# Output stores on another queue, a last tile in three parts, and weight pieces issued at other steps, in a hash-attention and gated feed-forward kernel

## The chip, the core and the metric

The kernel runs on one core of a Trainium2 chip. The metric is the device time of the whole program in microseconds (us), the median of five runs. The core has five engines with an instruction queue each: TensorE (PE in the profile), VectorE (DVE), ScalarE (ACT), GpSimd (POOL) and SyncE (SP). Each queue is worked off in its written order. DMA transfers are issued from SP, ACT and POOL and are carried by 16 DMA engines.

## The reference

For each of 4 batches and 8 heads, with 768 tokens of 64 features, queries and keys get a 6-bit bucket from the signs of a projection. A query attends only to keys of its own bucket. Then follows a gated feed-forward part on 3072 tokens of 512 features.

```python
q_bits = (np.einsum('bhsd,dk->bhsk', q, proj) > 0)
k_bits = (np.einsum('bhsd,dk->bhsk', k, proj) > 0)
mask = q_bucket[:, :, :, None] == k_bucket[:, :, None, :]
scores = np.where(mask, scale * np.matmul(q, k.transpose(0, 1, 3, 2)), -1e9)
x = softmax(scores) @ v                      # heads side by side: 3072 x 512
g, val = x @ w_gate, x @ w_val               # 512 -> 1536
ffn_out = (gelu(g) * val) @ w_out            # 1536 -> 512
out = x + sigmoid(x @ w_res) * ffn_out
```

## The kernel before, in words

The work is cut into eight blocks: 4 batches times 2 halves of 384 query tokens. In a block the 8 heads are taken as 4 pairs. A pair of a block has 6 steps; a block has 24.

One step computes scores for 2 key tiles of 128 and 384 queries (`scores`, L563 to L583): two matmuls into the double-buffered `sc`, and one exponential on ACT into `e`. The bucket mask is part of the matmul: `aug` holds, per head pair, 64 feature rows and 7 rows of bits, so that a pair of different buckets gets a very negative score. `attend` (L585 to L625) multiplies `e` with `vaug` (values with a column of ones) into the single-buffered `av`. After the sixth step of a pair DVE takes the reciprocal of the sums (L615) and writes the pair into `xtok` (L616); only then can the next pair use `av`. From the second block on, each pair's `xtok` is transposed by a DMA of the SP queue into `xT` (L624); in the first block PE does it (L638).

At the end of a block, `gate` (L648 to L661) multiplies `xT` with `wg` (12 column groups of 4 matmuls, L656) and ACT applies the gelu. `feed_forward` (L663 to L715) then multiplies with `wv` (L672), which DVE multiplies into `gh` (L675). For each of 3 token tiles there follow the gate product with `wr` (L684, ACT L687), 12 matmuls with `wo` (L697), two DVE operations into `y` and `o` (L705, L708), and the store of the tile (L714). In the last tile of the last block the 512 columns are done as two parts of 256. The feed-forward of one block is mixed between the attention steps of the next.

Head pairs reach `aug` in two ways. In the first batch (`prep_tokens`, L385 to L518) tokens are transposed on PE (L470, L494), the result is taken out of PSUM with a scale into `trT` (L395), hashed with a matmul (L457), turned into bits on DVE (L421), and moved into `aug` (L431), beside a cast of the features (L409 to L413). The table `EVAC` says which engine does the three takings-out of pairs 1 to 3: ACT for all. In later batches (`prep_blocks`, L520 to L552) tokens are loaded in pieces of 32 columns (L266), transposed on DVE (L526), hashed (L534), turned into bits (L541), and the bits are moved by DMAs of the POOL queue (L544). `cast_v` (L380), also on POOL, makes `vaug`.

The weights come through the POOL queue in 13 pieces (L361: `wg` 4, `wv` 4, `wr` 1, `wo` 4), with a cast on the way. The token loads of the second batch on SP wait until `wr` is there: `wait_weights` (L282) puts a tiny DMA in front of them that reads `wr` (L283).

What stands where in each queue is settled when the program is built. `arrange` (L136 to L257) is a planner: every operation has an engine, an estimated cost, its dependencies, its buffers (rings of the sizes in `RINGS`), and marks such as `margin` (an addition to the time at which it is taken to be ready). The planner plays this through and emits the operations in the order in which they start. Where PE has nothing to do during the first 35 us of the plan, it emits matmuls that do no useful work (L823, L826). So a change of one cost or one engine can move other instructions too.

Of the kernel before, what the change touches and what calls it, by code (L numbers as in the profile page):

```python
# [11 lines left out]
FP32 = mybir.dt.float32  # L12
# [8 lines left out]
def kernel(  # L21
# [12 lines left out]
    nc = tc.nc  # L34
    B, H, S, D = q.shape
# [34 lines left out]
                 th=2, y=2, o=2, rec=2)  # L70
# [312 lines left out]
    EVAC = [None] + [("ACT",) * 3] * 3  # L383

    def prep_tokens(n):  # L385
# [13 lines left out]
        def cast(eng, par, hhs, sides, after=()):  # L399
# [4 lines left out]
            def emit():  # L404
                do = {"DVE": nc.vector.tensor_copy, "ACT": nc.scalar.copy}[eng]
# [8 lines left out]
            op(eng, {"DVE": 0.16 + width * 0.00053, "ACT": 0.12 + width * 0.00088}[eng], emit,  # L414
               r=[(trT, hh, side) for hh in hhs for side in sides],
               w=[("aug", n % NAUG, hh, side, par, "d") for hh in hhs for side in sides], after=after)
# [46 lines left out]
        if n == 0:  # L463
            for hh in range(2):
                for side in range(2):
# [7 lines left out]
                    op("PE", 0.35, emit, r=[(st[side], hh)], w=[ps], margin=0.3 if hh else 0.0)  # L473
# [11 lines left out]
        else:  # L485

            tiles = [(hh, side, t2) for hh in range(2) for side in range(2) for t2 in range(TC)]
            for g in range(3):
# [8 lines left out]
                op("PE", 0.45, emit, r=[(st[side], 0) for side in range(2)], w=[ps], margin=0.4)  # L497
# [7 lines left out]
            for par in range(2):  # L505
                bit(hp, par, (0, 1))
            cast("DVE", 0, (0, 1), (0, 1))
            for hh in range(2):
                move(hh, 0, (0,))
                move(hh, 1, (0, 1))  # L510
                if hh == 0:
                    cast("DVE", 1, (0, 1), (1,))
# [150 lines left out]
    def feed_forward(u):  # L663
# [14 lines left out]
        for t in range(TC):  # L678
# [10 lines left out]
            parts = 2 if u == 2 * B - 1 and t == TC - 1 else 1  # L689
            W = DMODEL // parts  # L690
            for h in range(parts):
                cols = slice(h * W, (h + 1) * W)
                ps = bank()
                for k4 in range(KF // 4):
# [4 lines left out]
                    op("PE", 0.87 / parts, emit, r=[(g, kk) for kk in range(4 * k4, 4 * k4 + 4)] + [("wo", gg) for gg in range(KF // 3)],  # L699
# [3 lines left out]
                y = ring("y", [P, DMODEL], FP32)  # L703
                o = ring("o", [P, DMODEL], FP32)
                op("DVE", 0.66 / parts, lambda y=y, th=th, ps=ps, cols=cols, W=W: nc.vector.scalar_tensor_tensor(  # L705
                    y()[:, 0:W], th()[:, cols], 1.0, ps()[:, 0:W], op0=ALU.add, op1=ALU.mult), r=[th, ps], w=[y],
                   closes=("block", u + 1) if t == TC - 1 else None)
                op("DVE", 0.68 / parts, lambda y=y, o=o, t=t, cols=cols, W=W: nc.vector.scalar_tensor_tensor(  # L708
# [5 lines left out]
                op("SP", 0.5, lambda o=o, dst=dst, W=W: nc.sync.dma_start(dst, o()[:, 0:W]), r=[o], size=0.8)  # L714
# [13 lines left out]
    ahead = {0: (0, 0, 1, 1), 2: (2,), 5: (2,), 8: (3,), 11: (3,)}  # L728
    for i in range(LB):
# [5 lines left out]
        if i % 2 == 0:  # L735
            next(weights)
# [129 lines left out]
```

## Time and profile before

| quantity | us |
|---|---|
| median of 5 runs | 351.37 |
| lowest and highest of them | 349.91, 352.73 |
| the profiled execution's own time | 352.71 |
| its span, first to last instruction | 350.9 |
| PE busy in the span | 339.7 |
| ACT busy | 235.1 |
| DVE busy | 189.8 |
| POOL busy | 51.3 |

The span is what the profile's times count from. Some 1.8 us of the profiled execution lie outside it. A busy PE is not PE at its peak: matmuls are pipelined and their ends are modelled. Lines beginning with "PEld" are weight loads, which overlap matmuls. "SPq" and "POOLq" are the queues of these engines with their DMA issues.

### The profile page before, as it was taken

What the parts mean: (1) busy time and instruction counts of PE and PEld (TensorE: products, weight loads), DVE (VectorE), ACT (ScalarE), POOL (GpSimd) and SP (SyncE); (2) the same over time, 40 slices, a digit from 0 to 9 for tenths busy, and PEclk for the clock granted to TensorE, in tenths of its full rate; (3) what the DMA queues carried; (4) which work ended last, traced back from release to release, by engine and by line L of the source; (5) the groups of instructions that cost most, each with busy time, mean ns of one, the idle gap of its engine ahead of it and who ended that gap; (6) DMA issues with size and microseconds to landing.
All of it is one profiled execution on the core that took longest, in us unless ns stands there. A gap on an engine that the chain in (4) does not pass through costs nothing.

```text
span 350.9 us, 7702 instructions
## 1 busy us (share of the span) xinstructions
PE 339.7 (97%) x3073; PEld 202.5 (58%) x3097; DVE 189.8 (54%) x339; ACT 235.1 (67%) x341; POOL 51.3 (15%) x83
## 2 busy tenths in 40 slices
PE   8998999997999999999999999999999999999995
PEld 3666666454565556655666556555665556655653
DVE  3897137968389746896263534734162414423353
ACT  4789887653866758675876768685787758775410
POOL 0634000331234200302002100202000000000000
PEclk9999999998999999999999999999999999999999
DMA  7979999999987299863501120021000120012002
GB/s 225 350 156 186 206 152 160 136 156 177 185 138 125 67 184 151 144 140 81 111 12 19 45 75 2 16 55 48 30 13 13 43 73 0 20 48 71 2 0 90
DMA packets 117557, 34.23 MB, mean 98 GB/s; under 512 B 107786, under 2 KB 113554, under 8 KB 117522
## 3 DMA queue, kind: packets, MB, share of 16 engines
q1 hardware_dynamic: 112402, 27.78, 43.1%
q0 software_dynamic: 4816, 5.77, 9.2%
q8 instruction: 24, 0.39, 0.5%
q10 hardware_dynamic: 304, 0.20, 0.2%
q14 instruction: 11, 0.09, 0.1%
HBM read 29.36 MB, written 6.29 MB: 102 GB/s over the span
## 4 chain that ended last, share of the span: by engine, by line
PE 92%; DVE 4%; ACT 2%; DMA 1%; issue 1%; ACTq 0%
PE mm L656 18%; PE mm L672 18%; PE mm L697 18%; PE sc L574 16%; PE av L602 9%; PE mm L684 6%; PE mm L534 3%; ACT e L578 2%; DVE bits L421 1%; DVE aug L431 1%; PE idle L823 1%; DMA xT<-xtok 1%; PE mm L494 1%; PE mm L470 1%; PE av L826 1%
## 5 line engine op out<-in xcount | busy, mean ns | idle before, releaser
L578 ACT ACTIVATE e<-sc 128x768 bf16<-128x768 f32 x192 | 149.4, 810 | 52.4 <-PE sc L574 52.2
L675 DVE TENSOR_TENSOR gh<-mm,gh 128x384 bf16<-128x384 f32 x96 | 53.3, 556 | 79.9 <-PE mm L672 65.7
L574 PE MATMUL sc<-aug 71*128 71x384 bf16 x384 | 93.2, 327 | 1.0 <-ACT e L578 0.7
L672 PE MATMUL mm<-xT,wv 128*128 128x384 bf16 x384 | 73.5, 326 | 0.0
L602 PEld LDWEIGHTS <-e 128*128 128x128 bf16 x1152 | 57.1, 97 | 23.4 <-PE mm L494 1.1
L656 PE MATMUL mm<-xT,wg 128*128 128x384 bf16 x384 | 67.5, 330 | 2.6 <-DMA xT<-xtok 2.4
L697 PE MATMUL mm<-wo,gh 128*128 128x512 bf16 (+1 forms) x291 | 69.0, 371 | 0.4
L660 ACT ACTIVATE gh<-mm 128x384 bf16<-128x384 f32 x96 | 45.4, 490 | 34.8 <-PE mm L656 34.5
L602 PE MATMUL av<-vaug,e 128*128 128x65 bf16 x1152 | 62.4, 194 | 1.3 <-DVE xtok L616 1.3
L656 PEld LDWEIGHTS <-wg 128*128 128x128 bf16 x384 | 37.4, 99 | 28.4 <-issue 4.4
L574 PEld LDWEIGHTS <-aug 71*128 71x128 bf16 x384 | 34.8, 99 | 29.3 <-issue 5.7
L672 PEld LDWEIGHTS <-wv 128*128 128x128 bf16 x384 | 34.0, 98 | 21.5 <-issue 3.1
L544 POOL DMA_DIRECT2D aug<-bits x48 | 27.1, 570 | 103.3 <-DVE bits L541 103.1
L697 PEld LDWEIGHTS <-gh 128*128 128x128 bf16 x300 | 26.9, 98 | 26.1 <-issue 1.9
L705 DVE SCALAR_TENSOR_TENSOR y<-th,mm 128x512 f32<-128x512 bf16 (+1 forms) x25 | 16.6, 665 | 46.8 <-PE mm L697 41.7
L380 POOL CAST vaug<-vs 128x768 bf16<-128x768 f32 x16 | 15.4, 965 | 87.3 <-DMA vs<-in_v_dram 58.5
L687 ACT ACTIVATE th<-mm 128x512 bf16<-128x512 f32 x24 | 14.3, 597 | 16.6 <-PE mm L684 16.6
L549 DVE TENSOR_SCALAR aug<-trT 64x1536 bf16<-64x1536 f32 x24 | 23.4, 975 | 1.1 <-PE sc L574 0.4
L684 PE MATMUL mm<-wr,xT 128*128 128x512 bf16 x81 | 22.9, 380 | 0.8
L541 DVE TENSOR_SCALAR bits<-mm,shift 128x384 bf16<-128x384 f32 x24 | 13.6, 609 | 10.4 <-PE mm L534 10.3
L616 DVE TENSOR_TENSOR xtok<-av,rec 128x384 bf16<-128x384 f32 x32 | 17.8, 557 | 1.1
L708 DVE SCALAR_TENSOR_TENSOR o<-y,xtok 128x512 f32<-128x512 f32 (+1 forms) x25 | 17.1, 685 | 0.9
(54 smaller groups left out, 152.3 us busy)
## 6 DMA issues: line engine op xcount, KB each, us to landing
vs<-in_v_dram SPq DMA_DIRECT2D x16, 384.0 KB
out_dram<-o SPq DMA_DIRECT2D x23, 256.0 KB
qs<-in_q_dram SPq DMA_DIRECT2D x48, 96.0 KB
ks<-in_k_dram SPq DMA_DIRECT2D x48, 96.0 KB
wg<-in_moe_w_gate_dram POOLq DMA_DIRECT2D x4, 384.0 KB, 8.1
wv<-in_moe_w_val_dram POOLq DMA_DIRECT2D x4, 384.0 KB, 6.7
wo<-in_moe_w_out_dram POOLq DMA_DIRECT2D x4, 384.0 KB, 14.9
qs<-in_q_dram SPq DMA_DIRECT2D x3, 384.0 KB
```

Of the source, the lines that this page charges most:

```text
L544: op("POOL", 0.6, lambda i=i: nc.gpsimd.dma_start(a[D:KAUG, :, i * CH:(i + 1) * CH], bits()[32 * i:32 * i + NR]), r=[(bits, 0), (bits, 1)] ...
L549: lambda hh=hh: nc.vector.tensor_scalar_mul(a[0:D, hh, :], trT()[hh * D:(hh + 1) * D].rearrange("d s n -> d (s n)"), QKS),
L574: nc.tensor.matmul(sp()[:, x, 0:CH], a[:, S + jt * P:S + (jt + 1) * P], a[:, c * CH:(c + 1) * CH], start=True, stop=True)
L578: op("ACT", 0.72, lambda: nc.scalar.activation(e(), sp()[:, :, 0:CH], AF.Exp, scale=EXPS), r=[sp], w=[e], table="exp", held=True, opens=(" ...
L602: nc.tensor.matmul(av()[:, o:o + D + 1], e()[:, x, t * P:(t + 1) * P], va[:, 2 * j + hh, TS[b][jt], :], start=(first and x == 0 and t == 0 ...
L616: op("DVE", 0.48, lambda: nc.vector.tensor_mul(xt()[:, j].rearrange("p t (h d) -> p h t d", h=2), view()[:, :, :, 0:D], rec().to_broadcast ...
L656: nc.tensor.matmul(ps()[:, 0:CH], wg[:, kk, m * P:(m + 1) * P], x()[:, kk, :], start=(kk == 0), stop=(kk == KM - 1))
L660: op("ACT", 0.385, lambda: nc.scalar.activation(g()[:, m, :], ps()[:, 0:CH], AF.Gelu), r=[ps], w=[(g, m)], table="gelu", closes=("gelu", u ...
L672: nc.tensor.matmul(ps()[:, 0:CH], wv[:, kk, m * P:(m + 1) * P], x()[:, kk, :], start=(kk == 0), stop=(kk == KM - 1))
L675: op("DVE", 0.46, lambda m=m, ps=ps: nc.vector.tensor_mul(g()[:, m, :], ps()[:, 0:CH], g()[:, m, :]), r=[ps], w=[(g, m)])
L684: nc.tensor.matmul(rps(), x()[:, kk, t * P:(t + 1) * P], wr[:, kk, :], start=(kk == 0), stop=(kk == KM - 1))
L697: nc.tensor.matmul(ps()[:, 0:W], g()[:, kk, t * P:(t + 1) * P], wo[:, kk, cols], start=(kk == 0), stop=(kk == KF - 1))
```

## The change

1. The stores of blocks 1 to 7 (21 stores of 128 x 512) are issued from the POOL queue. Those of the last block stay on SP.
2. The last tile of the last block is done in parts of 256, 128 and 128 columns, with buffers `yz` and `oz` of their own, three each.
3. The 13 weight pieces are planned at steps 3, 4, 6, 7, 9, 10, 12, 13, 15, 16, 18, 19 and 21 of the first block, where they were planned at every second step from 0 to 24.
4. In pairs 1 to 3 the second of the three takings-out of `trT` is done by DVE (`EVAC`).
5. Margins change: for the transposes of the keys of head 1 of pair 0 from 0.3 to 1.3, and of pairs 1 and 2 from 0.4 to 1.4.
6. Planner costs of the two last DVE operations and of the store change. The tables `MOVER` and `CASTER` are new and name DVE everywhere, as before.

```diff
-    EVAC = [None] + [("ACT",) * 3] * 3
+    EVAC = [None, ("ACT", "DVE", "ACT"), ("ACT", "DVE", "ACT"), ("ACT", "DVE", "ACT")]
+    MOVER = ["DVE", "DVE", "DVE", "DVE"]
+    CASTER = [None, ("DVE", "DVE"), ("DVE", "DVE"), ("DVE", "DVE")]
...
-                    op("PE", 0.35, emit, r=[(st[side], hh)], w=[ps], margin=0.3 if hh else 0.0)
+                    op("PE", 0.35, emit, r=[(st[side], hh)], w=[ps], margin=(0.3, 1.3)[side] if hh else 0.0)
...
-                op("PE", 0.45, emit, r=[(st[side], 0) for side in range(2)], w=[ps], margin=0.4)
+                op("PE", 0.45, emit, r=[(st[side], 0) for side in range(2)], w=[ps], margin=(None, 1.4, 1.4, 0.4)[n])
...
-            parts = 2 if u == 2 * B - 1 and t == TC - 1 else 1
-            W = DMODEL // parts
-            for h in range(parts):
-                cols = slice(h * W, (h + 1) * W)
+            parts = [256, P, P] if u == 2 * B - 1 and t == TC - 1 else [DMODEL]
+            for h, W in enumerate(parts):
+                cols = slice(sum(parts[:h]), sum(parts[:h]) + W)
...
-                y = ring("y", [P, DMODEL], FP32)
-                o = ring("o", [P, DMODEL], FP32)
-                op("DVE", 0.66 / parts, lambda ...
+                z = "z" if len(parts) > 1 else ""
+                y = ring("y" + z, [P, parts[0]], FP32)
+                o = ring("o" + z, [P, parts[0]], FP32)
+                op("DVE", 0.1 + 0.56 * W / DMODEL, lambda ...
...
-                op("SP", 0.5, lambda o=o, dst=dst, W=W: nc.sync.dma_start(dst, o()[:, 0:W]), r=[o], size=0.8)
+                eng, queue = ("SP", nc.sync) if u == 2 * B - 1 else ("POOL", nc.gpsimd)
+                op(eng, 0.6, lambda o=o, dst=dst, W=W, queue=queue: queue.dma_start(dst, o()[:, 0:W]), r=[o], size=0.8)
...
+    WSTEPS = (3, 4, 6, 7, 9, 10, 12, 13, 15, 16, 18, 19, 21)
...
-        if i % 2 == 0:
+        if i in WSTEPS:
             next(weights)
```

## The prediction

> **What bounds the kernel now.** I read the page's busy times first, then PE's waits, the stage table, and the queues around the largest wait.
>
> ```profile
> span 350.9 us, 7702 instructions
> PE 339.7 (97%) x3073; PEld 202.5 (58%) x3097; DVE 189.8 (54%) x339; ACT 235.1 (67%) x341; POOL 51.3 (15%) x83
> ```
>
> PE is idle for only 11.2 us in all, so a gain must come from those, from useless or slow PE work, or from the two ends. PE's waits have one large entry:
>
> ```profile
> PE mm L656 <- DMA xT<-xtok: 2.4, 1, 2.4
> PE av L602 <- DVE xtok L616: 1.3, 2, 0.9
> ```
>
> The stage table around it (length, busy time and count of PE, PEld, DVE, ACT, POOL; then PE's granted clock, DMA share, GB/s):
>
> ```profile
> 78.00:80.00 2.00, 0.82 (x5) 0.39 (x4) 1.69 (x3) 0.00 (x0) 0.00 (x0) 1.00 1.18 298
> 80.00:82.00 2.00, 0.80 (x3) 0.41 (x3) 1.99 (x2) 0.00 (x0) 1.39 (x1) 0.76 0.69 195
> 82.00:85.00 3.00, 3.00 (x19) 1.57 (x18) 2.93 (x5) 0.40 (x2) 0.00 (x0) 0.59 0.82 133
> ```
>
> The wait ends at 81.2, and the clock is low until about 85: the stall costs more than its 2.4 us. It is at the gate of block 2, which needs the transposes of pairs 3 and 4. The SP queue then:
>
> ```profile
> 75.99 0.73 SPq L266 DMA_DIRECT2D vs<-in_v_dram  x1
> 76.83 1.17 SPq L714 DMA_DIRECT2D out_dram<-o  x1
> 78.09 1.23 SPq L624 DMA_TRANSPOSE xT<-xtok  x1
> 79.42 0.52 SPq L714 DMA_DIRECT2D out_dram<-o  x1
> 80.03 1.20 SPq L624 DMA_TRANSPOSE xT<-xtok  x1
> ```
>
> Pair 3 was in `xtok` at 68.2, but its transpose was issued at 78.09, behind loads and a store. SP issues without a pause from 38.16 to 81; what started it is SP's longest early wait:
>
> ```profile
> SPq L283 <- DMA wr<-in_moe_w_res_dram: 10.2, 1, 10.2
> ```
>
> POOL and the DMA engines before that (timeline, then a stage row):
>
> ```profile
> 23.43 1.36 POOL L380 CAST vaug<-vs 128x768 bf16<-128x768 f32 x1 [6.01 <-DMA vs<-in_v_dram]
> 24.73 2.19 POOL L361 DMA_DIRECT2D wv<-in_moe_w_val_dram  x4
> 26.87 0.81 POOL L361 DMA_DIRECT2D wr<-in_moe_w_res_dram  x1
> ...
> 24.00:26.00 2.00, 2.00 (x40) 1.13 (x25) 1.95 (x4) 1.32 (x3) 2.00 (x4) 1.00 0.12 23
> ```
>
> `wv` and `wr` stand behind a cast that waits for the fourth `vs`; meanwhile the DMA engines run dry (share 0.12). After 85 each stage of about 40 us has 0.15 us of idle PE, so only the first 85 us and the tail can change much.
>
> **The change part by part.** *Weight pieces.* In the changed program POOL's queue reads: cast, cast, `wg`, cast, three `wg`, cast, then `wv`, `wr`, `wo`; before it was cast, two `wg`, two casts, two `wg`, cast. So the first two pieces, issued at 11.36 to 12.6, fall behind the casts of the second and third `vs`: estimate 14.3 and 15.8. Until then the token loads have the DMA engines alone. Stage rows put 3.25 MB into SBUF by 12 us; the tokens of the first batch are 12 x 393 KB = 4.72 MB; the rest at the 396 GB/s of 10 to 12 us takes 3.7 us, plus some 1.5 us to land: the fourth `vs` is there at about 17 instead of 23.4, and `wv` is issued from about 18.5. Then no gap forms. Between 22.5 and 26 the finer rows are 178, 89, 61, 0, 49 and 131 GB/s in slices of 0.75 us, where a `wg` or `wv` stream makes 215: (6 - 508/215) x 0.75 = 2.7 us lost. So `wr` lands at 38.2 - 2.7 = 35.5 and the SP chain starts 2.7 us earlier. Bounds: no gain, if the total is set by something else, and 3.9 us, from counting bytes at full rate. I take 2.7. `wg` itself lands near 25 and is first used at about 38, `wv` at 46: covered.
>
> *Stores.* SP loses 1.17 + 0.52 us and two gaps of 0.09: the transpose of pair 3 moves up 1.26 us for the store alone, that of pair 4 1.87 us. With the chain 2.7 us earlier pair 3 is issued at 78.1 - 1.3 - 2.7 = 74.1; pair 4 must wait for its `xtok` (76.0 before, 75.6 below), so it is issued at 75.7 and, at 3.1 us from issue to use as in the chain of waits (78.09 3.07), lands at 78.8. PE, now with all four score matmuls ahead, comes to the gate at 78.4 and needs pair 4 after nine matmuls of 0.163, at 79.8. Margin 1 us: the stall is gone. Worth: from the start of the last `wo` group (75.41) to the long gate run (85.14) it is 9.73 us; in block 3, where nothing stalls, 121.79 to 127.17 = 5.38, plus 0.19 for six `av` matmuls that lie elsewhere. Saving 9.73 - 5.57 = **4.2 us**.
>
> [...] The rows show 0.76 and 0.59 after a 2.4 us wait; they decide, and I keep 4.2.
>
> POOL pays 21 issues. Nearest row, also from POOL:
>
> ```profile
> L544 POOL DMA_DIRECT2D aug<-bits x48 | 27.1, 570 | 103.3 <-DVE bits L541 103.1
> ```
>
> 21 x 0.6 = 13 us on an engine that spends 103 us waiting for bits. What is queued behind a store are the `vaug` casts and these bit moves. [...] L544 took at most 0.89 here beside busy DVE. [...]
>
> *DVE for ACT in the first block.* ACT loses 3 x 0.60 us (L395). DVE gains three of about 0.69 (L395 at 384 columns is 0.552 and L705 grows from 0.42 to 0.686 for 256 columns). Neither counts alone, because DVE closes each pair (L615, L616) after it has done the next pair's bits. Walking the new order with the old durations (exponential 0.74 apart, cast 0.95 and 0.56, two bits 1.14, four moves 1.3, closing 0.8):
>
> ```profile
> 15.75 1.14 DVE L421 TENSOR_SCALAR bits<-mm,shift 128x384 bf16<-128x384 f32 x2
> 16.93 1.32 DVE L431 COPY aug<-bits 7x384 bf16<-7x384 bf16 x4
> ...
> 22.64 0.56 DVE L616 TENSOR_TENSOR xtok<-av,rec 128x384 bf16<-128x384 f32 x1
> ```
>
> The key transposes of head 1 now stand behind a hash that waits for `proj` until 7.45, so the first exponential slips from 10.3 to about 11.1. The moves of pair 2 end at 18.4 (18.25 before), exponential 8 is done at 20.7 (21.1), number 11 starts at 23.7 (25.2). Then DVE's extra work tells: pair 1 is closed at 24.1 (23.2), number 13 starts at 25.7 (26.7); pair 2 is closed at 29.6 (28.95), number 19 starts at 31.2 (31.6). Eight more at 0.74 and the last end at 37.8 instead of 38.18: **-0.4 us**. Bounds: -1.8, if all of ACT's time were a gain, and +2.1, if all of DVE's were a loss. [...]
>
> *Tail.* Two halves took 2.78 us of PE; 12 matmuls of 256 (1.39) and 24 of 128 (0.061 each, as the 116-column L826) make 2.85. DVE then is the limit: with 0.285 for a 128-column operation its last one ends at 347.95, before at 347.91. A smaller last store may give 0.1 back. **0**; bounds -0.3 and +0.3.
>
> **Sum.** -4.2 - 0.4 + 0 = -4.6 on a span of 350.9 gives 346.3; with the 1.8 us around it the profiled execution's 352.71 becomes 348.1. That execution was 1.3 us above the median; on the median of 351.37 the same difference gives **346.8 us**.
>
> **The rivals.** *Store and loads share the DMA engines (B).* The chain from 38.16 on is paced by transfers, and `wr` lands as late as before because bytes are bytes. [...] For it: DMA shares over 1 in 55 to 75. Against: 298 GB/s at 78 to 80, so 125 to 160 is not full, and the gap at 24 to 26.
>
> *The gate of the loads opens later (C), slower.* Place: the SP wait on `wr`. The first pieces are issued 3 to 4 us later; if that lateness goes through the 13-piece queue instead of filling the gap, `wr` lands at 42, the chain moves +3.8, the stores give back 1.3, and the transpose is 2.5 us later: 353.9. It decides from `wr` at about 39.5. Against: the old order itself left the engines empty.
>
> *DVE becomes the bound of the first block (D).* The stall goes, but the first block is 2.1 us longer: 351.4 - 4.2 + 2.1 = 349.3. For it: DVE was busy 22.0 of 28.35 us there. *The whole 1.8 us of ACT is gained (E):* 345.4.
>
> **How the numbers follow.** Chances: the main case 0.55, B 0.19, C 0.12, D 0.08, E 0.06. Half a per cent, 1.76 us, is about what a measurement of this kernel can tell from no change: the bounds are 349.6 and 353.1. Faster: main, E, D and a part of B, 0.72; same: most of B and a little of C, 0.17; slower: 0.11. The main case alone spans 345.0 to 348.9, from the bounds of the first block. For 8 in 10 the range takes in D and most of B, and a little of E: 344.7 to 350.9. C is left out.
>
> **What would show it.** `wv` issued near 18.5 to 20 and SP's tiny read of `wr` near 35.5; no wait of L656 for `xT` and no slice of low clock near 80; the first gelu table load near 37.8; `aug` issues still under 0.9 us; last DVE operation 3 us before the end. The prediction is wrong if `wr` lands at 38 or later, if the fourth `vs` still lands after 20, or if the first exponentials fall into groups with gaps over 1 us.

## The result

The changed kernel takes 349.84 us (median of 43 executions, 348.41 to 352.04) against 350.4 us of the kernel before (80 executions, 348.01 to 354.02): a ratio of 0.9983, interval 0.9969 to 0.9996. Forecast were 346.8 us and a range of 344.7 to 350.9. The time lies in the range, but the gain is 0.6 us where 4.6 were forecast, so the forecast was wrong in size: a gain of over one per cent was forecast, and what came can hardly be told from none. A ratio is not the quotient of the two medians, and it leaves out executions more than 1.5% above the fastest of their kernel.

The profiled execution of the changed kernel took 349.84 us. Lines of the changed kernel have other numbers: L581 is the scores, L585 the exponential, L609 `attend`, L623 the closing of a pair, L631 the transpose, L663 the gate, L703 the `wo` matmuls, L722 the store. From its page, the head and the busy times:

```profile
span 348.0 us, 7654 instructions
PE 335.8 (96%) x3044; PEld 199.6 (57%) x3068; DVE 191.9 (55%) x344; ACT 233.7 (67%) x338; POOL 64.5 (19%) x104
```

POOL has the 13 us of stores that were forecast, and PE is idle for 12.2 us, 1.0 us more than before, although the span is 2.9 us shorter. PE's waits, largest first (total, times, longest, us):

```profile
PE mm L663 <- DMA xT<-xtok: 2.6, 2, 1.8
PE sc L581 <- ACT e L585: 1.4, 5, 0.4
PE av L609 <- DVE xtok L623: 1.2, 1, 1.2
PE sc L581 <- DVE aug L434: 0.4, 1, 0.4
```

In this execution the wait for the transposed pair is not gone. It is one wait of 1.8 us in place of 2.4, and a second one of 0.8 us has come. The stage rows around the first (columns as in the prediction):

```profile
78.00:80.00 2.00, 0.22 (x2) 0.00 (x0) 1.93 (x4) 1.76 (x2) 0.94 (x2) 1.00 1.13 84
80.00:82.00 2.00, 2.00 (x23) 1.34 (x23) 1.99 (x2) 0.50 (x2) 0.46 (x1) 1.00 1.16 233
82.00:85.00 3.00, 3.00 (x25) 1.83 (x21) 2.93 (x4) 2.22 (x5) 0.00 (x0) 1.00 1.34 161
```

PE has 0.22 us of work from 78 to 80, but the clock stays at 1.00 behind it. That gives most of the shorter span of this execution: from the first gate matmul to the long gate run the chain of waits has 45.05 us (37.43 to 82.48) against 46.92 before, and the low rows of before had cost (1 - 0.76) x 2 + (1 - 0.59) x 3 = 1.7 us of PE's time. The SP queue (start, duration):

```profile
72.42 0.46 SPq L266 DMA_DIRECT2D vs<-in_v_dram  x1
72.98 3.08 SPq L631 DMA_TRANSPOSE xT<-xtok  x1
76.15 2.29 SPq L631 DMA_TRANSPOSE xT<-xtok  x1
```

From the chain of waits, the same transpose from issue to landing:

```profile
72.98 6.98 DMA xT<-xtok
```

Pair 3's transpose is issued 5.1 us earlier than before (72.98 for 78.09) and lands 1.2 us earlier (79.96 for 81.16). Its issue lasts 3.08 us where it lasted 1.23, and the way from issue to landing takes 6.98 us where it took 3.07. The second wait, in PE's timeline:

```profile
202.43 0.65 PE L663 MATMUL mm<-xT,wg 128*128 128x384 bf16 x3
203.89 0.65 PE L663 MATMUL mm<-xT,wg 128*128 128x384 bf16 x3 [0.81 <-DMA xT<-xtok]
```

POOL's timeline ahead of it:

```profile
196.85 2.19 POOL L551 DMA_DIRECT2D aug<-bits  x4 [5.09 <-DVE bits L548]
199.04 0.58 POOL L722 DMA_DIRECT2D out_dram<-o  x1
```

A store stands behind four bit moves and goes out at 199.04, beside the transpose of that block, which is issued at 199.06 and lands at 203.85, 4.79 us later.

The early weights went as forecast on POOL (start, duration):

```profile
17.95 0.83 POOL L380 CAST vaug<-vs 128x768 bf16<-128x768 f32 x1
18.71 2.63 POOL L361 DMA_DIRECT2D wv<-in_moe_w_val_dram  x4
21.32 0.79 POOL L361 DMA_DIRECT2D wr<-in_moe_w_res_dram  x1
```

but SP's tiny read of `wr` goes out at 36.99 (38.16 before, 35.5 forecast). ACT in the first block does what the prediction named as its own refutation, exponentials in groups with a gap of over 1 us (start, duration, count, and the idle time before):

```profile
25.11 0.81 ACT L585 ACTIVATE e<-sc 128x768 bf16<-128x768 f32 x1 [1.11 <-PE sc L581]
26.53 3.70 ACT L585 ACTIVATE e<-sc 128x768 bf16<-128x768 f32 x5 [0.61 <-PE sc L581]
30.64 5.91 ACT L585 ACTIVATE e<-sc 128x768 bf16<-128x768 f32 x8 [0.41 <-PE sc L581]
36.78 0.81 ACT L585 ACTIVATE e<-sc 128x768 bf16<-128x768 f32 x1 [0.23 <-ACT e L585]
37.61 1.28 ACT L667 ACT_TABLE_LOAD   x1
```

From the first exponential (9.36) to the load of the gelu table it is 28.25 us; before it was 27.90 (10.30 to 38.20).

### The profile page after: what moved, and what is told of

The parts are those of the page before. It is cut to its first block, busy times and chain, and to the rows that moved or that the text cites. A ratio compares the mean times of both kernels' runs of the same rounds, so it can differ in the third digit from the quotient of the medians.

```text
span 348.0 us, 7654 instructions
## 1 busy us (share of the span) xinstructions
PE 335.8 (96%) x3044; PEld 199.6 (57%) x3068; DVE 191.9 (55%) x344; ACT 233.7 (67%) x338; POOL 64.5 (19%) x104
## 4 chain that ended last, share of the span: by engine, by line
PE 87%; DVE 5%; DMA 3%; ACT 2%; issue 1%; DVEq 0%; ACTq 0%
PE mm L679 18%; PE mm L663 17%; PE sc L581 16%; PE mm L703 16%; PE av L609 9%; PE mm L691 5%; DMA xT<-xtok 3%; PE mm L541 3%; ACT e L585 2%; DVE bits L424 1%; DVE aug L434 1%; PE idle L832 1%; PE mm L460 1%; PE mm L473 0%; DVE xtok L623 0%
## 5 line engine op out<-in xcount | busy, mean ns | idle before, releaser
L585 ACT ACTIVATE e<-sc 128x768 bf16<-128x768 f32 x192 | 149.4, 809 | 54.9 <-PE sc L581 54.5
L581 PE MATMUL sc<-aug 71*128 71x384 bf16 x384 | 92.0, 326 | 1.9 <-ACT e L585 1.4
L609 PEld LDWEIGHTS <-e 128*128 128x128 bf16 x1152 | 56.5, 97 | 23.3 <-DVE xtok L623 2.2
L703 PE MATMUL mm<-wo,gh 128*128 128x512 bf16 (+2 forms) x303 | 69.0, 363 | 0.4
L663 PE MATMUL mm<-xT,wg 128*128 128x384 bf16 x384 | 66.2, 326 | 2.8 <-DMA xT<-xtok 2.6
L609 PE MATMUL av<-vaug,e 128*128 128x65 bf16 x1152 | 61.8, 194 | 1.2 <-DVE xtok L623 1.2
L663 PEld LDWEIGHTS <-wg 128*128 128x128 bf16 x384 | 37.0, 98 | 28.1 <-issue 3.5
L581 PEld LDWEIGHTS <-aug 71*128 71x128 bf16 x384 | 34.8, 98 | 29.7 <-issue 5.0
L703 PEld LDWEIGHTS <-gh 128*128 128x128 bf16 x312 | 27.2, 98 | 26.0 <-issue 1.9
L712 DVE SCALAR_TENSOR_TENSOR y<-th,mm 128x512 f32<-128x512 bf16 x23 | 15.8, 686 | 45.2 <-PE mm L703 40.1
L722 POOL DMA_DIRECT2D out_dram<-o x21 | 13.0, 619 | 112.1 <-DVE rec L622 81.9
L556 DVE TENSOR_SCALAR aug<-trT 64x1536 bf16<-64x1536 f32 x24 | 24.1, 1005 | 1.1 <-PE sc L581 0.4
L380 POOL CAST vaug<-vs 128x768 bf16<-128x768 f32 x16 | 14.2, 888 | 51.4 <-DMA vs<-in_v_dram 37.1
L623 DVE TENSOR_TENSOR xtok<-av,rec 128x384 bf16<-128x384 f32 x32 | 17.8, 557 | 1.1
```

Of the source, the lines that this page charges most:

```text
L556: lambda hh=hh: nc.vector.tensor_scalar_mul(a[0:D, hh, :], trT()[hh * D:(hh + 1) * D].rearrange("d s n -> d (s n)"), QKS),
L581: nc.tensor.matmul(sp()[:, x, 0:CH], a[:, S + jt * P:S + (jt + 1) * P], a[:, c * CH:(c + 1) * CH], start=True, stop=True)
L585: op("ACT", 0.72, lambda: nc.scalar.activation(e(), sp()[:, :, 0:CH], AF.Exp, scale=EXPS), r=[sp], w=[e], table="exp", held=True, opens=(" ...
L609: nc.tensor.matmul(av()[:, o:o + D + 1], e()[:, x, t * P:(t + 1) * P], va[:, 2 * j + hh, TS[b][jt], :], start=(first and x == 0 and t == 0 ...
L623: op("DVE", 0.48, lambda: nc.vector.tensor_mul(xt()[:, j].rearrange("p t (h d) -> p h t d", h=2), view()[:, :, :, 0:D], rec().to_broadcast ...
L663: nc.tensor.matmul(ps()[:, 0:CH], wg[:, kk, m * P:(m + 1) * P], x()[:, kk, :], start=(kk == 0), stop=(kk == KM - 1))
```

## The experiments

Times are medians; ratios are against the kernel before, run on the same chip. Each run also lists the mean granted clock of the whole execution. These means fall into two groups with nothing between 0.995 and 0.997: executions at 0.997 or more, and executions at 0.995 or less. In six of the seven profiles that show a low clock, its slices add up to 1.7 us of lost PE time, which is 3.4 us at a clock of 0.50 (81.0 to 84.4 us in the profile of before) and makes 0.995 of 350 us; in the seventh they add up to 3.4 us (mean 0.990). The latter are called "with a half clock stretch" below, and the shares of them turned out to tell more than the medians.

**One part of the change at a time, added to the kernel before.**

Stores of all blocks but the last on the Pool queue:

```diff
-                op("SP", 0.5, lambda o=o, dst=dst, W=W: nc.sync.dma_start(dst, o()[:, 0:W]), r=[o], size=0.8)
+                eng, queue = ("SP", nc.sync) if u == 2 * B - 1 else ("POOL", nc.gpsimd)
+                op(eng, 0.6, lambda o=o, dst=dst, W=W, queue=queue: queue.dma_start(dst, o()[:, 0:W]), r=[o], size=0.8)
```

> The kernel before with the stores of blocks 1 to 7 on the POOL queue, nothing else. The forecast's theory (SP's issue order sets when the transposes land): pair 3's transpose moves up 1.3 us and pair 4's 1.9 us, so the time falls by 1.3 to 1.9 us. Transfer theory (transposes land when the DMA engines have carried what is in flight, and a store issued from POOL at the same moment competes with them): the pair-4 transpose lands less than 0.5 us earlier, the time changes by -0.5 to +0.8 us, and a wait of the gate matmuls for xT of 0.5 to 1 us may appear in a later block, where store and transpose now start together (as at 203 us in the changed kernel).

Measured: 351.7 us (14 executions), ratio 1.003 (0.9992 to 1.0068); a half clock stretch in 8 of 14. From its SP queue:

```profile
75.56 0.68 SPq L266 DMA_DIRECT2D vs<-in_v_dram  x1
76.34 3.23 SPq L624 DMA_TRANSPOSE xT<-xtok  x2
```

and from its chain of waits:

```profile
76.34 4.27 DMA xT<-xtok
```

The transpose is issued 1.75 us earlier than before and lands 0.55 us earlier, at 80.61. Counted from the end of the last load's issue to the landing it is 4.37 us without the store (76.24 to 80.61) and 4.44 with it in before (76.72 to 81.16): the store between them had cost the landing next to nothing. PE waits as long as before, and here the clock stays at 1.00 behind the wait:

```profile
80.66 0.81 PE L656 MATMUL mm<-xT,wg 128*128 128x384 bf16 x4 [2.40 <-DMA xT<-xtok]
```
```profile
80.00:82.00 2.00, 1.34 (x9) 0.81 (x9) 1.95 (x3) 0.00 (x0) 1.15 (x2) 1.00 0.68 196
82.00:84.00 2.00, 2.00 (x19) 1.28 (x18) 1.97 (x3) 1.28 (x4) 0.00 (x0) 1.00 1.07 172
```

Moving the stores alone gains nothing.

The weight pieces issued later:

```diff
+    WSTEPS = (3, 4, 6, 7, 9, 10, 12, 13, 15, 16, 18, 19, 21)
...
-        if i % 2 == 0:
+        if i in WSTEPS:
```

> The kernel before with the weight pieces at the new steps, nothing else. Forecast's theory: wv is issued near 18.5 us, wr lands 2.7 us earlier than 38.2, the wait for xT near 80 us nearly goes: -2 us or more. Transfer theory: wv is issued near 18.7 but wr lands only about 1.2 us earlier (the carried bytes set it), and the time falls by 0.5 to 1.2 us.

Measured: 348.85 us (22 executions), ratio 0.9951 (0.9932 to 0.9971); a half clock stretch in 1 of 22. SP's queue in its profile, with the stores still on it:

```profile
72.34 0.47 SPq L266 DMA_DIRECT2D vs<-in_v_dram  x1
72.91 1.26 SPq L714 DMA_DIRECT2D out_dram<-o  x1
74.26 1.22 SPq L624 DMA_TRANSPOSE xT<-xtok  x1
```

and from the chain of waits:

```profile
74.26 3.42 DMA xT<-xtok
```

Issued 1.3 us later than in the changed kernel, the transpose lands 2.3 us earlier, at 77.68, and PE waits 0.2 us. So here a store between the loads and the transpose did not make the transpose late. The weights alone bring more than the whole change does.

The last tile in parts of 256, 128 and 128 columns with own buffers (the first lines of that hunk; it also carries the planner's new costs, 0.6 for 0.5 for every store on SP):

```diff
-            parts = 2 if u == 2 * B - 1 and t == TC - 1 else 1
+            parts = [256, P, P] if u == 2 * B - 1 and t == TC - 1 else [DMODEL]
```

> The kernel before with the last tile in parts of 256, 128 and 128 with own buffers, nothing else. Forecast: 0 (bounds -0.3 to +0.3). From the changed kernel's trace (last DVE operation 0.19 us earlier against the start of the tile, 2.59 instead of 2.99 us from there to the end): -0.6 us.

Measured: 349.17 us (22 executions), ratio 0.9967 (0.9943 to 0.9991); a half clock stretch in 5 of 22; PE's wait for the pair 1.7 us. The tail forecast at nothing has a gain in it: from the last tile's first output matmul to the end of the span it is 6.35 us here and 6.71 before. That is a third of the 0.33%; the planner also put some loads, stores and a transpose of a later block in another order on SP.

The evacuations (the takings-out of `trT`) on DVE and the planner's margins, the lines of the margins cut to that argument:

```diff
-    EVAC = [None] + [("ACT",) * 3] * 3
+    EVAC = [None, ("ACT", "DVE", "ACT"), ("ACT", "DVE", "ACT"), ("ACT", "DVE", "ACT")]
...
-margin=0.3 if hh else 0.0)
+margin=(0.3, 1.3)[side] if hh else 0.0)
...
-margin=0.4)
+margin=(None, 1.4, 1.4, 0.4)[n])
```

> The kernel before with the second of three takings-out on DVE and the new margins, nothing else. Forecast's theory for this part: -0.4 us at the gelu of the first block (bounds -1.8 to +2.1). If transfers pace the chain from wr to the transposes, what the first block gains is waited for again at the gate near 80 us and the time changes by less than 0.3 us either way.

Measured: 350.24 us (14 executions), ratio 0.9981 (0.9952 to 1.001); a half clock stretch in 8 of 14. In the profile it lies at 30 to 34 us (clock 0.57 and 0.58), in the first block, and not at 80. In this kernel the executions with a stretch are no longer than those without (medians of 350.21 and 350.28 us).

**The change with parts of it left out.** All but the stores, which stay on SP:

```diff
-                eng, queue = ("SP", nc.sync) if u == 2 * B - 1 else ("POOL", nc.gpsimd)
-                op(eng, 0.6, lambda o=o, dst=dst, W=W, queue=queue: queue.dma_start(dst, o()[:, 0:W]), r=[o], size=0.8)
+                op("SP", 0.6, lambda o=o, dst=dst, W=W: nc.sync.dma_start(dst, o()[:, 0:W]), r=[o], size=0.8)
```

> The changed kernel with all stores back on SP; weight steps, takings-out, margins and tail stay. If moving the stores costs time (transfer theory), this is faster than the changed kernel by 1 us or more: the three parts alone gave ratios 0.9951, 0.9967 and 0.9981, together about 0.990, some 347 us, and PE's wait for xT at the second gate is under 0.5 us. If instead the parts get in each other's way without the stores, it stays near the changed kernel's 349.8 us.

Measured: 349.89 us (22 executions), ratio 0.9986 (0.9964 to 1.0008), as the change itself; a half clock stretch in 9 of 22, in the profile at 30 to 34 us, right behind a slice with 1.26 us of PE work in 2. PE does not wait for a transposed pair anywhere in this profile: the transpose of pair 3 is issued behind a store at 74.81, in 1.22 us, and lands 4.44 us later, at 79.25, and PE, late from the first block, comes to the gate at 80.85.

Weights and tail together, on the kernel before (the two diffs above):

> The kernel before with the new weight steps and the new tail only. Sum of the two parts alone: ratio 0.992, some 347.6 us. If the takings-out and margins bring something of their own beside these, this is slower than the kernel with all but the stores by 0.5 us or more; if not, equal within 0.5 us.

Measured: 348.99 us (22 executions), ratio 0.9964 (0.9942 to 0.9986); no half clock stretch in 22. It is no better than the weights alone; the parts do not add. In its profile pair 3's transpose is issued at 76.77 (74.26 with the weights alone) and PE waits 1.6 us for it, at full clock.

The change without the three stores of block 1, so that nothing at all is stored beside the transposes (block 1's rows of the output stay unwritten):

```diff
-                op(eng, 0.6, lambda o=o, dst=dst, W=W, queue=queue: queue.dma_start(dst, o()[:, 0:W]), r=[o], size=0.8)
+                if u > 0: op(eng, 0.6, lambda o=o, dst=dst, W=W, queue=queue: queue.dma_start(dst, o()[:, 0:W]), r=[o], size=0.8)
```

> The changed kernel without the three stores of block 1 (their rows of the output are left unwritten). If the store that POOL issues at 74.65 us slows the transposes that SP issues at 72.98 and 76.1, pair 3 lands at about 77 instead of 79.96, PE's wait at this gate goes and the time falls by about 1.5 us. If the transposes are slow because they stand one right behind the other, or because of the loads ahead of them in SP's ring, pair 3 still lands near 80 and the wait stays at 1.5 to 2 us.

Measured: 349.36 us (12 executions), ratio 0.9995 (0.9963 to 1.0026); a half clock stretch in 7 of 12. The transpose behind the loads is issued at 72.75, the next one after a pause at 76.55, and their issues last 2.57 and 2.23 us without any store near; the first lands 6.71 us after its issue. So it is not the stores' bytes that hold them.

The change with only block 1's stores on the Pool queue:

```diff
-                eng, queue = ("SP", nc.sync) if u == 2 * B - 1 else ("POOL", nc.gpsimd)
+                eng, queue = ("POOL", nc.gpsimd) if u == 0 else ("SP", nc.sync)
```

> The changed kernel with only the stores of block 1 on POOL and all others on SP. If the wait for xT at 203 us (0.81 us) comes from store and transpose starting at the same moment, it goes, and the time falls by 0.5 to 0.8 us; the wait at the second gate stays at 1.5 to 2 us. If the wait at 203 us is independent of the store's queue, it stays.

Measured: 349.02 us (20 executions), ratio 0.9963 (0.9939 to 0.9988); a half clock stretch in 8 of 20. There is no wait for a transposed pair in the profile, neither near 80 nor at 203.

**Where the half clock comes from.** A second profiled execution of the kernel before:

> The kernel before once more, for a second profiled execution. Theory: the order on the queues is the same, so TensorE waits 2.0 to 2.6 us again for pair 3's transpose near 79 us, but no half clock follows it (79 of 121 executions of before showed a mean clock of 0.9965 or more): time about 349.6. Rival (the half clock is this wait's own price): a wait over 2.2 us is again followed by 0.5 to 0.8 clock within 4 us, and the time is about 352.

Measured: 352.6 us, with the larger wait and a half clock right behind it; the rival's forecast. PE's wait:

```profile
PE mm L657 <- DMA xT<-xtok: 2.7, 1, 2.7
```

and the stage rows around it:

```profile
78.00:80.00 2.00, 0.25 (x1) 0.10 (x1) 1.95 (x3) 0.00 (x0) 1.05 (x1) 0.75 0.91 269
80.00:82.00 2.00, 2.00 (x8) 0.94 (x7) 1.97 (x3) 0.00 (x0) 0.00 (x0) 0.50 0.57 100
82.00:84.00 2.00, 2.00 (x15) 1.14 (x14) 1.97 (x3) 0.86 (x3) 0.00 (x0) 0.50 0.98 157
84.00:86.00 2.00, 2.00 (x15) 1.07 (x13) 0.99 (x2) 0.68 (x3) 0.00 (x0) 0.54 1.18 156
```

Both profiles of before have the low clock there. But it isn't in every execution: beside these experiments 80 of 211 executions of before have a half clock stretch (median 352.19 us) and 131 have none (349.68).

The change with evacuations and margins as before (the fourth diff above, reversed):

> The kernel after with the three evacuations and the planner's margins as before; weights, tail and all stores on the Pool queue stay. Theory (the short stretch of half clock comes where TensorE has just been short of work, and the moved evacuations make such a stretch at 20 to 30 us in the first block): it now falls in at most 1 execution in 10, as with the weights alone (1 of 22) and weights with tail (0 of 22), against 14 of 43 after; the median drops to that of the undisturbed executions of after, about 349.2 to 349.4, and those undisturbed ones themselves gain nothing. Rival (the half clock comes from the wait at 80 us or from the stores on Pool, as 8 of 14 with the stores alone suggest): its share stays at a third or more, median 349.8 or above.

Measured: 348.41 us (6 executions), ratio 0.991 (0.9868 to 0.9951); no half clock stretch in 6. The share fell as the theory said. The executions without a stretch, which it expected to gain nothing, took 348.41 us against 349.42 of the changed kernel, but these are only six executions.

The same with only block 1's stores on the Pool queue:

> Weights and tail as after, evacuations and margins as before, and only block 1's three stores on the Pool queue. Theory (each part keeps what it showed): half clock in at most 1 execution in 10, no second wait for a transposed pair at 203 us, and the block 1 wait shorter than 1.8 us; median 348.2 to 348.5, below both kernels and below weights with tail (348.99). Rival (the parts do not add, since each moves the same first 80 us about): 348.9 to 349.2, no better than weights with tail.

Measured: 348.28 us (6 executions), ratio 0.9903 (0.9863 to 0.9944); no half clock stretch in 6; the wait for the pair 0.9 us.

Which of the two it is. The change with only the margins taken back, evacuations on DVE (the lines cut to that argument):

```diff
-margin=(0.3, 1.3)[side] if hh else 0.0)
+margin=0.3 if hh else 0.0)
...
-margin=(None, 1.4, 1.4, 0.4)[n])
+margin=0.4)
```

> The kernel after with only the planner's two margins as before; the moved evacuations stay, and the plan has 30 filler matmuls in the first block. Theory (the evacuation on DVE is what costs: it takes the filler and delays DVE): half clock in a third or more, median 349.6 to 350.3. Rival (the margins are what costs): half clock in at most 1 in 10, median 348.2 to 348.8.

Measured: 351.0 us (22 executions), ratio 1.0024 (1.0001 to 1.0046), and a half clock stretch in 18 of 22. But this run doesn't part the two: without the margins the planner puts the pieces of `wg` back where they were, POOL's fourth cast waits until 23.83 again, and SP's read of `wr` goes out at 40.23. So the margins are what the weights' new place hangs on. The stage rows of its first block:

```profile
28.00:30.00 2.00, 1.20 (x6) 0.29 (x4) 1.91 (x5) 2.00 (x4) 2.00 (x4) 1.00 1.05 194
30.00:32.00 2.00, 1.69 (x26) 1.52 (x27) 1.97 (x5) 0.58 (x1) 0.45 (x1) 0.60 1.04 197
32.00:34.00 2.00, 2.00 (x23) 1.49 (x22) 0.46 (x3) 1.32 (x2) 0.76 (x1) 0.55 1.11 217
```

From 28 to 30 PE has six matmuls to do and waits for the exponentials and then for DVE's closing of a pair (PE's timeline):

```profile
28.45 0.48 PE L581 MATMUL sc<-aug 71*128 71x384 bf16 x2 [0.22 <-ACT e L585]
29.19 0.49 PE L581 MATMUL sc<-aug 71*128 71x384 bf16 x2 [0.26 <-ACT e L585]
30.31 1.47 PE L609 MATMUL av<-vaug,e 128*128 128x65 bf16 x24 [0.63 <-DVE xtok L623]
```

The change with only the evacuations back on ACT, margins kept:

```diff
-    EVAC = [None, ("ACT", "DVE", "ACT"), ("ACT", "DVE", "ACT"), ("ACT", "DVE", "ACT")]
+    EVAC = [None] + [("ACT",) * 3] * 3
```

> The kernel after with only the three evacuations back on ACT; the two margins stay, and the plan has 72 filler matmuls in the first block. Theory (the evacuation on DVE is what costs): half clock in at most 1 in 10, median 348.2 to 348.8, as with both taken back (348.41). Rival (the margins are what costs): half clock in a third or more, median 349.6 to 350.3.

Measured: 348.84 us (22 executions), ratio 0.9952 (0.9933 to 0.9971); no half clock stretch in 22. POOL's fourth cast is at 18.53 here (17.95 in the change), so the weights keep their new place and the evacuations are what differs, with what the planner makes of them: 72 filler matmuls in the first block for 28. Two of the same slices:

```profile
28.00:30.00 2.00, 2.00 (x38) 1.60 (x34) 1.95 (x4) 1.96 (x3) 0.52 (x2) 1.00 1.10 216
30.00:32.00 2.00, 1.72 (x23) 1.12 (x20) 0.75 (x2) 2.00 (x4) 0.42 (x1) 1.00 1.06 207
```

and ACT's exponentials:

```profile
9.57 0.81 ACT L585 ACTIVATE e<-sc 128x768 bf16<-128x768 f32 x1 [0.71 <-PE sc L581]
24.25 12.54 ACT L585 ACTIVATE e<-sc 128x768 bf16<-128x768 f32 x17 [0.88 <-PE sc L581]
36.81 1.28 ACT L667 ACT_TABLE_LOAD   x1
```

The last 17 exponentials run without a gap, and from the first one to the table load it is 27.24 us, 1.0 us less than in the change. That pair flatters it. Over all profiles with the weights later, the same stretch is 27.2 to 29.2 us with the evacuations on ACT (six) and 28.3 to 28.9 on DVE where no half clock fell into it (four); on DVE with a half clock in it, it is 29.3 to 30.2 (five, old order of the weights included).

The change with twice the filler matmuls in the first block:

```diff
-                for _ in range(2):
+                for _ in range(4):
                     nc.tensor.matmul(live[0]()[:, 2 * TC * DV:512], warm[:, 0:P], warm[:, 0:512 - 2 * TC * DV],
```

> The kernel after, with four filler matmuls in place of two wherever the planner puts filler in the first block: 56 of them in place of 28, no other instruction changed or moved. Theory (half clock comes for want of filler where TensorE waits in the first block): executions with a mean clock of 0.995 or less fall from a third to at most 1 in 10; undisturbed executions lose up to 0.7 us by the filler that stands ahead of real work; median 349.2 to 349.9. Rival (the moved evacuation brings the half clock by its waits, filler or not): a third or more still have it, median 349.8 to 350.5.

Measured: 349.4 us (14 executions), ratio 0.9972 (0.9944 to 1.0); a half clock stretch in 8 of 14. Stage rows:

```profile
22.00:24.00 2.00, 0.67 (x19) 0.53 (x18) 1.94 (x5) 1.53 (x3) 0.91 (x2) 1.00 1.08 200
24.00:26.00 2.00, 2.00 (x31) 0.50 (x27) 1.55 (x3) 0.81 (x1) 1.01 (x1) 0.70 1.07 207
```

The share did not fall, as the rival said, but the run does not decide between the two. The planner places filler where its plan has PE idle, and the real wait is elsewhere: in this run no filler stands between 13.2 and 33.7 us, and in the change none between 12.7 and 32.9, whereas with the evacuations on ACT 39 filler matmuls start between 14 and 33 us. So PE has 0.67 us of work in two, and then the half clock; filler in that stretch was not tried.

**The transposes behind the loads.** The change with the nine loads that stand ahead of them issued on the Pool queue (the planner also moved one transpose back to the other two):

```diff
-                    load(nm, "SP", g, s, lambda t, g=g: t[g:g + Q],
+                    load(nm, "POOL" if n == 7 else "SP", g, s, lambda t, g=g: t[g:g + Q],
-                         src[b, 2 * j + hh, :, c * Q:(c + 1) * Q].rearrange("(m p) d -> p m d", p=Q), 0.8, 0.85, True)
+                         src[b, 2 * j + hh, :, c * Q:(c + 1) * Q].rearrange("(m p) d -> p m d", p=Q), 0.8, 0.85, n != 7)
-        load("v", "SP", 0, s, lambda t: t, v[b, 2 * j:2 * j + 2].rearrange("h (t p) d -> p h t d", p=P), 1.8, held=True)
+        load("v", "POOL" if n == 7 else "SP", 0, s, lambda t: t, v[b, 2 * j:2 * j + 2].rearrange("h (t p) d -> p h t d", p=P), 1.8, held=n != 7)
```

> The kernel after with the nine loads of one head pair that stand on SP right ahead of block 1's last transposes issued on the Pool queue instead; the same bytes go at about the same time. Theory (a transpose issued on SP right behind a run of loads is held by SP's own queue): the transposes of block 1 issue in 1.2 us each and land within 3.2 us of it, before 78 us; no wait for them near 80 us; long gate run at 80.5 to 81 in place of 82.3, time 1 to 1.5 us below after, 348.4 to 348.8. Rival (they share the DMA engines with the loads, whichever queue these are on): issue to landing stays at 4 to 7 us, and the time within 0.5 us of after's.

Measured: 350.29 us (6 executions), ratio 0.995 (0.9907 to 0.9993); a half clock stretch in 4 of 6. The transpose that now stands first behind loads takes 4.46 us to issue (65.07), the next two 1.21 and 1.20. The last of them is issued at 74.83, as soon as its pair is there, and still takes 4.82 us to land; PE waits 0.8 us. So each side has half, by one profile: the long issue goes with the place right behind the loads, the long way to landing doesn't go away with it.

**Against the change itself, on one chip.** The changed kernel once more, and the change with the evacuations on ACT and only block 1's stores on the Pool queue:

> The kernel after once more, beside the next one on the same chip. Theory: 349.6 to 350.1 as before, mean clock 0.995 or less in about a third of its executions; in this profile either no half clock or one that follows a short-of-work stretch of TensorE between 20 and 30 us. Rival (the first measurement of after was a draw of the chip): 348.4 to 349.0 as without the evacuations on DVE.

> The kernel after with the evacuations back on ACT and only block 1's three stores on the Pool queue; weights, tail and margins stay. Theory: no half clock, 348.2 to 348.8, 0.3 to 0.4 per cent below the kernel after and the fastest of all. Rival (which stores are on the Pool queue is of no matter): within 0.2 us of 348.85, where all stores but the last block's are on it.

Measured: 349.56 us (12 executions, 5 with a half clock stretch), ratio 0.9982 (0.9953 to 1.0012), and 349.08 us (12, none), ratio 0.9944 (0.9914 to 0.9974). The direction is the expected one, but the two intervals overlap and 0.5 us is less than the spread of either; and 349.08 is no better than with all stores on the Pool queue (348.84), so which stores are moved isn't seen to matter. In this second profile of the changed kernel the wait near 80 us is gone: the transpose, issued at 72.45, lands at 78.91, and PE comes to the gate at 79.12. What is left is the wait at 203:

```profile
PE mm L664 <- DMA xT<-xtok: 0.8, 1, 0.8
```

## Why the prediction was wrong

The half clock first, by groups of kernels:

| kernels | executions | with a half clock stretch |
|---|---|---|
| before | 211 | 80 |
| before with the stores on the Pool queue | 14 | 8 |
| before with the new tail | 22 | 5 |
| those with evacuations on DVE (nine runs, the changed kernel in two) | 165 | 81 |
| the six with the weights later and evacuations on ACT | 90 | 1 |

In both profiles of before the stretch lies behind the wait at 80 us. In all five profiles of kernels with evacuations on DVE that have one, it lies between 24 and 34 us.

Point by point, by the prediction's own steps:

- **The stall, forecast -4.2: the step that failed most.** It has two terms, 2.4 us of wait and 1.8 us of clock loss, and both were too large. The clock term took the one profiled execution for the typical one. The loss is real there, but only 80 of 211 executions have it; the median of before lies 0.77 us above the 349.68 us of those without, so no more than that was to be had from it. And the wait alone does not bring it: with the stores alone moved PE waited 2.40 us at the same place at full clock. The wait term took 3.1 us from issue to use from a transpose that stood behind a store. In the new order it stands right behind nine loads, where issue and landing together took 6.98 us (6.46 in the second profile). Of the earlier issue, 5.1 us, only 1.2 arrived. Of the 1.26 us that the step gave to the stores next to nothing arrived when they were moved alone. "The stall is gone" holds in one of the two profiles of the change, but there PE comes to the gate later; the end of the stall moved from 81.20 and 79.75 us (before, twice) to 80.00, and without a wait to 79.12. The profile of before had the warning: its own transpose right behind loads took longer to issue, and by the trace's semaphores it landed 5.46 us after its start.

```profile
66.26 2.15 SPq L624 DMA_TRANSPOSE xT<-xtok  x1
```

- **Weight pieces.** The mechanism was right: `wv` was issued from 18.71 (18.5 forecast), no gap of the DMA engines followed, and this edit alone brought 0.49%. The 1.5 us to land in its walk stand in no row (a bit move on POOL took 1.7 us at the least); the fourth cast began at 17.95. The size was off: SP's read of `wr` goes out at 36.99, and in the thirteen profiles of kernels with the pieces later in POOL's order at 35.5 to 38.6, in the middle 36.6; in five with the old order at 37.3 to 38.9, in the middle 38.2 (a sixth, with the margins taken back, has 40.23). That is 1.6 us, not 2.7. The six slices that the step sums reach to 27 us, not 26; the sum stands.
- **DVE for ACT in the first block, forecast -0.4 (bounds -1.8 and +2.1).** This step had the wrong sign. With these three evacuations back on ACT and all else kept, 348.84 us (ratio 0.9952, 0.9933 to 0.9971) and no half clock in 22; with them, 349.84 (0.9983, 0.9969 to 0.9996) and 14 of 43. The sum has no term for the clock of the first block, where the change has 28 filler matmuls and before had 70. With the weights later, 55 of 129 executions with the evacuations on DVE have the stretch and 1 of 90 with them on ACT. How much of the 1.0 us is there without any half clock is not settled: executions of the changed kernel that have none take 349.42 us (29), but those of the change with only block 1's stores moved, evacuations on DVE too, take 348.27 (12), less than the 348.85 of the kernel with them on ACT, which ran on another chip. The walk of the new order ended close, at 37.8 us for the last exponential (37.59 measured), by luck: two errors stand against each other. The first exponential came at 9.36 and not at 11.1, and from it to the table load it took 28.25 us where the walk has 26.7. The groups of exponentials before 30.6 wait for PE; from 30.64 on they run at 0.74 us each, as walked. Rival D (DVE becomes the bound, 349.3) had the place; its size came near, but as a half clock in some executions. Whether the missing filler or the waits for DVE bring the half clock is not parted: both come with the evacuations on DVE, and filler was never put into the stretch from 14 to 33 us.
- **Tail, forecast 0 (bounds 0.3 each way).** In the profiles the last tile's first output matmul to the last DVE operation's end took 3.51 us (3.70 before), and from there to the end 2.6 us (3.0): together -0.6. With the tail alone it is 6.35 us in place of 6.71, with the stores alone 6.53, so some 0.35 us come from the tail and 0.2 from the stores that left SP. The last operation, in the change and before:

```profile
345.12 0.29 DVE L715 SCALAR_TENSOR_TENSOR oz<-yz,xtok 128x128 f32<-128x128 f32 x1
```
```profile
347.49 0.42 DVE L708 SCALAR_TENSOR_TENSOR o<-y,xtok 128x256 f32<-128x256 f32 x1
```

- **POOL pays at no cost.** Right for block 1: 21 issues took 13.0 us, mean 619 ns; the longest store issue took 1.17 us, the longest bit move 1.01. Whether the wait of 0.8 us at 203 belongs to it isn't settled: both profiles of the changed kernel have it, those with only block 1's stores moved don't, but neither do four in which all are moved, and one with every store on SP has 0.3 us of it.
- **Rival B**, that bytes are bytes, came closest in time, by luck: with 1.3 us for the stores and 0.4 for the first block as the whole gain, 351.37 becomes 349.7, but the 1.3 us did not come. With the stores alone moved the transpose was issued 1.75 us earlier, and from the last load's issue to the landing it took 4.37 us in place of 4.44. The premise that `wr` lands as late as before was wrong by 1.2 us. Rival C's sign, `wr` from 39.5 us on, did not come (36.99).
- **The price of the low clock** was taken from the rows, rightly for what one execution shows: a half clock did follow 2.4 and 2.7 us of waiting twice. But waits of 2.40, 2.16, 1.78, 1.68 and 1.63 us at the same gate passed without it in other kernels' profiles. What the rows did not give was how often. A sum over medians needs that share.

An account of the 4.0 us that are missing (-4.6 forecast, -0.6 measured), an estimate from two profiles of each kernel. Clock: forecast -1.8; the median of before stands 0.77 us above its executions without a half clock stretch, that of the changed kernel, over both its runs, 0.26 (349.71 and 349.45, 55 executions), so -0.5 came, 1.3 are missing. Wait: forecast -2.4; PE's waits for the pair sum to 2.6 and 0.8 us in the two profiles of the changed kernel and to 2.4 and 2.7 in those of before, so between +0.2 and -1.9 came, 0.5 to 2.6 are missing. First block: from the first exponential to the table load 28.25 and 28.89 us in the change and 27.90 and 27.58 in before, +0.3 to +1.3 instead of -0.4, 0.7 to 1.7 missing. Tail: 0.6 more than forecast. 1.3 + (0.5 to 2.6) + (0.7 to 1.7) - 0.6 is 1.9 to 5.0, which holds the 4.0; single executions differ by 1 us and more, so it doesn't go finer.

**What stays open.** Weights alone gave -0.49%, the tail alone -0.33%, both together -0.36%; why they don't add was not found (the tail's edit also moves SP's order through the planner's cost of a store). Why a transpose right behind loads takes longer to issue and to land was narrowed, not settled: not the stores' bytes (they were left out), and only in part the loads on SP's own queue (they were moved). That the half clock in the first block comes with the evacuations on DVE is shown by the shares; that PE's lack of work is its reason is argued from where it lies, and it wasn't produced by an idle stretch alone.

## What to carry to other kernels

Before a stall is priced with the low clock behind it, ask for the clock of many executions: here the profiled one had it and the typical one hadn't, and the share of executions with it, 0 of 22 against 14 of 43 for one line of a table, pointed to the culprit where medians 1 us apart hardly did. A transfer that is issued earlier hasn't landed earlier (here 5.1 us at the issue became 1.2 at the landing): take issue-to-landing from a transfer with the same neighbours ahead of it on its queue, because a store that looks like an obstacle may cost the landing next to nothing (4.44 us with it, 4.37 without). Before filler, or anything else that is tried against a low clock, is called useless, look whether it went into the stretch that was ill (with the filler doubled, none stood between 13.2 and 33.7 us, and the half clock began between 24 and 26). And work that is moved to an engine that closes each step isn't free because both totals look so: with the three takings-out on DVE it was 349.84 us, on ACT 348.84. That it is paid in the wait for the closing was not shown: PE's waits for it sum to 1.2 us in the one profile and to 1.0 in the other.

## What the runs showed of the hardware

- A granted clock of 0.50 came in stretches of 3.4 us (81.0 to 84.4 us in the profile of before; a loss of 1.7 us of PE's time in six profiles, of twice that in one), in some executions of a program and not in others, with the same instructions. It began within or right behind spells in which PE had little to do: waits of 2.38 and 2.68 us, or 1.20 us of work in 2 us with no single wait over 0.63 us. It did not follow waits of 2.40, 2.16, 1.78, 1.68 and 1.63 us in other profiles, nor 0.83 us of work in 2 in the changed kernel (22 to 24 us).
- Executions with a stretch were 2.5 us longer in before (352.19 against 349.68), whose two profiles have it at the gate of block 2, and 1.3 us longer in the changed kernel (350.78 against 349.45); with only evacuations and margins changed there was no difference (350.21 against 350.28).
- A transpose by DMA in the first 85 us took 1.2 us to issue behind a store (13 in all nineteen profiles) and 1.5 to 4.5 us right behind a run of loads on the same queue (49). By the semaphores in the traces, it took 2.3 to 4.6 us from issue to landing behind a store and 3.9 to 8.6 us right behind loads. Behind a pause or another transpose the issue took 1.2 to 2.3 us.
